# Token tile transposes, w_out rows and a scale chain at other places of one kernel's program order

## The chip, the core and the metric

The kernel runs on one core of a Trainium2 chip. Its engines work side by side, each through its own queue in order: PE (matrix products into PSUM), DVE and ACT (elementwise work, ACT also the GELU), POOL and SP (here mostly issuing transfers; ACT issues some too). The metric is the device time of one execution in microseconds (us). Times inside the profiled execution count from the start of its span.

## The reference

The input x has 2048 tokens of 576 channels. All is float32.

```python
h = _layernorm(x) * (1 + ca) + sa
x = x + ga * _A_ref(h, ...)              # a state-space convolution over the tokens
h = _layernorm(x) * (1 + cb) + sb
z = _gelu(einsum("bsd,df->bsf", h, w_in))          # 576 -> 4608
z1, z2 = z[..., :2304], _layernorm(z[..., 2304:])
g = einsum("ts,bsf->btf", w_sp, z2) + b_sp[None, :, None]   # 2048 x 2048 over the tokens
x = x + gb * einsum("bsf,fd->bsd", z1 * g, w_out)  # 2304 -> 576
```

The kernel computes each large product from float16 pairs: a tensor is split into a high part (a rounded copy, made by ACT) and a low part (the rest, made by DVE), and three products of the parts are summed.

## The kernel before

Three stages follow one another. The first, the state-space part, is not touched.

**The token stage** (`phase_a`) goes over 16 tiles of 128 tokens. For tile b:

- `ln2_rows(b)` (DVE) makes the normalized rows n; it runs two tiles ahead, and lets go the buffer of the token load `x1t`, for which the next load on SP (`x1_load`) waits.
- `turn(b)` (PE) transposes n in five pieces into `pt`, a PSUM tile of which there is one. `turn_hi(b)` (ACT, two instructions) copies it to the high part of `nt`, `turn_lo(b)` (DVE, two) makes the low part, and issues its store `n_d` on POOL. There are three nt.
- `z2_mm(b, h)` (PE) for h = 0 to 4: 14 products each of nt with a strip of w_in, into `pz`, of which there are six. The first four need the high part, and so do the next four; the low part comes after that.
- `z2_gelu(b, h)` (ACT) writes pz through the GELU to z. A tile's z takes two buffers of four, so that tile b's first GELU waits until the store of tile b - 2 (`z_d`) has landed.
- `z2_stats` and `roots` (DVE) make mean and scale (`nm`, `r`) of z; roots is a chain of some 17 tiny instructions, followed, for odd b, by `z2_diff`, which forms a difference of z's two halves. `z2_norm` (ACT) then normalizes z, and `z2_store` (POOL) stores it. For tile b - 1 all this runs inside tile b.

Between these, weights for later are prepared: `do(b, k)` runs the side jobs of tile b at place k. Place A0 stands ahead of a tile's first GELU; there ACT forms sums of squares of loaded weights (`wsst`, `wst`), and waits for their loads. The whole stage is pinned: each engine runs its instructions in the order in which the code names them.

After tile 15, its last statistics, roots, norm and store follow outside the loop.

**The first block** (`first_block`) makes the first 512 tokens of g. Its loop runs over nine column blocks f, called pairs here. For each pair PE multiplies w_sp with four sets, `zset` (set 4f + i), 42 products each (`g_products`); `part(f, i)` is the work of ACT and DVE that goes beside set i. A set is loaded from z_d into `raw`, gets three sums (DVE), a high part (ACT) and a low part (DVE, 2.0 us); there are three buffers, and the sets are made two ahead. Part 0 of a pair also takes the pair before through its sums (`gt`, six DVE instructions) and its product with z1. In pairs 1 to 6 PE has two units of z1 products besides (`ps<-n2q,wf`); four units stand ahead of pair 0. In the parts 1 to 3 rows of w_out are split, one a part (`wout_hi` on ACT, `wout_lo` on DVE, then the load of a later row on SP). The scales of the next block (`roots_sp(1)`, `scales_gate(1)`) are a chain of 20 tiny DVE instructions. ACT issues the stores of two sets out of three in its own queue (`set_d`), each behind the low part of its set.

After pair 8 the output product with w_out follows, and then three more blocks of the same kind; both are not touched.

The lines of the profile are those of a helper (L222) nearly everywhere, so instructions are told apart by their tiles.

Of the kernel before, what the change touches and what calls it, by code (L numbers as in the profile page):

```python
# [914 lines left out]
class Mlp:  # L915
# [466 lines left out]
    def phase_a(self):  # L1382
        self.n2o, self.n2t, self.wrs = {}, {}, {}
        self.prods, self.z1s, self.n2, self.bsp, self.gbs, self.wfs = {}, {}, {}, {}, {}, {}
        ap = self.ap = self.pool(self.c2, "ap", 2)
        cpa = ExitStack()
        self.pa = self.pool(cpa, "pa", 6, space=PSUM)
        self.ps1 = lambda: self.pa.tile([128, 512], F32, name="pz")
        self.zp = self.pool(self.c2, "zp", 2)
        self.wp = self.pool(self.ctx, "wp", 7, side="right")  # L1390

        self.bq = self.pool(self.ctx, "bq", 1, side="right")
        self.cfp = self.ctx.enter_context(ExitStack())
        self.fp = self.pool(self.cfp, "fp", 1, side="right")
        self.wso = ap.tile([128, 4, 10, 128], F16, name="wso", bufs=1)
        self.nc, plain = self.tied, self.nc
        self.nc.vector.memset(self.wso[64:, :, 9], 0.0)

        LD, PE, A0, A1, V0, V1 = range(6)
        sides = [[[] for _ in range(6)] for _ in range(17)]  # L1400

        def side(b, k, fn, *a):
            sides[b][k].append((fn, a))

        def do(b, k):
            for fn, a in sides[b][k]:
                fn(*a)

        for q in range(5):
            side(2 * q, LD, self.side_load, q)  # L1410
            side(2 * q + 1, A0, self.side_sum, q)
            side(2 * q + 1, PE, self.win_scale, q)
            side(2 * q + 1, A1, self.side_hi, q)
            side(2 * q + 1, V1, self.side_last, q)
            side(2 * q + 1, V1, self.side_lo, q, 0)
            side(2 * q + 2, V0, self.side_lo, q, 1)
        for h in range(2):
            side(1, LD, self.bsp_load, ap, h)
            side(2, A0, self.norm_bsp, h)
        for i in range(8):  # L1420
            side(2 + i // 2, A1, self.wsp_load, 0, i, ap)
            side(3 + i // 2, A0, self.norm_sp, 0, i)
        for i in range(12):
            side(6 + i // 2, A1, self.out_load, ap, i)
            side(7 + i // 2, A0, self.norm_out, i)
        for i in range(6):
            side(12 + i // 2, A1, self.wsp_load, 1, i, ap)
            side(13 + i // 2, A0, self.norm_sp, 1, i)
        side(13, V1, self.sums_out)
        side(14, PE, self.scales_out)  # L1430
        side(6, V1, self.sums_sp, 0)
        side(7, PE, self.scales_sp, 0)
        side(11, PE, self.scales_gate, 0)
        side(12, PE, self.scale_p, 0)
        for i in range(7):
            side(9 + i, V0, self.wsp_sums, i)
            side(9 + i, A1, self.wsp_hi, 0, i)
            side(9 + i, V1, self.wsp_lo, 0, i)
            side(8 + i, V1, self.block_load, 0, i)
        side(12, LD, self.z1_rows, 0)  # L1440
        side(14, LD, self.bias_load, 0)
        for f, b in ((0, 14), (9, 15), (1, 15)):
            side(b, LD, self.z1_load, 0, f)


        self.turn(0)
        self.turn_hi(0)
        self.x1_load(4)
        self.turn_lo(0)
        do(0, LD)  # L1450
        self.z2_mm(0, 0)
        do(0, A0)
        self.z2_gelu(0, 0)
        self.ln2_rows(1)
        do(0, PE)
        self.z2_mm(0, 1)
        self.z2_gelu(0, 1)
        self.start_sum(4)
        self.z2_mm(0, 2)
        self.turn(1)  # L1460
        self.start_lo(3)
        self.win_scale(9)
        self.turn_hi(1)
        self.start_hi(4)
        self.turn_lo(1)
        do(0, V0)
        self.z2_gelu(0, 2)
        self.z2_mm(0, 3)
        do(0, A1)
        self.start_lo(4)  # L1470
        self.ln2_rows(2)
        self.z2_stats(0, 0, 1, 2, 3)
        self.z2_gelu(0, 3)
        self.ln2_stats(3)
        do(0, V1)
        self.z2_stats(0, 4)
        self.z2_mm(0, 4)
        self.z2_gelu(0, 4)
        for b in range(1, 16):
            do(b, LD)  # L1480
            self.z2_mm(b, 0)
            do(b, A0)
            self.z2_gelu(b, 0)
            self.z2_stats(b - 1, 5)
            self.roots(b - 1, b + 2 if b + 2 < 16 else None)
            if b % 2:
                self.z2_diff(b - 1)
            self.z2_norm(b - 1)
            if b + 2 < 16:
                self.ln2_rows(b + 2)  # L1490
            if b + 4 < 16:
                self.x1_load(b + 4)
            self.z2_mm(b, 1)
            if b + 1 < 16:
                self.turn(b + 1)
            do(b, PE)
            self.z2_gelu(b, 1)
            self.z2_store(b - 1)
            do(b, V0)
            self.z2_stats(b, 0, 1)  # L1500
            if b + 1 < 16:
                self.turn_hi(b + 1)
            if b + 1 < 16:
                self.turn_lo(b + 1)
            self.z2_mm(b, 2)
            self.z2_gelu(b, 2)
            do(b, A1)
            self.z2_mm(b, 3)
            self.z2_stats(b, 2, 3)
            self.z2_gelu(b, 3)  # L1510
            if b + 3 < 16:
                self.ln2_stats(b + 3)
            do(b, V1)
            self.z2_stats(b, 4)
            self.z2_mm(b, 4)
            self.z2_gelu(b, 4)
        cpa.close()
        self.z2_stats(15, 5)
        self.roots(15)
        self.z2_norm(15)  # L1520
        self.z2_store(15)
        self.nc = plain
        self.c2.close()
# [497 lines left out]
    def first_block(self, order):  # L2021
# [16 lines left out]
        def sums(n):  # L2038
            if n < 36:
                self.z2_sums(n)  # L2040
# [13 lines left out]
        def part(f, i):  # L2054

            n = 4 * f + i
            if i == 0 and f:
                gate[:] = self.g_unit(0, f - 1, pgs.pop())
                gate[0]()
                hi(n + 2)  # L2060
                lo(n + 2)
                load()
                gate[1]()
                if f < 7:
                    z1()
                    z1()
                gate[2]()
                store(n + 2)
                sums(n + 4)
            if i:  # L2070
                if i == 1 and f:
                    gate[3]()
                if 2 <= f < 8:
                    k = next(rows)
                    self.wout_hi(k)
                    self.wout_lo(k)
                if f:
                    sums(n + 4)
                if (f, i) == (0, 3):
                    z1()  # L2080
                    z1()
                hi(n + 2)
                if i == 1 and f:
                    gate[4]()
                if not f:
                    sums(n + 3)
                lo(n + 2)
                load()
                store(n + 2)
                if i == 1 and f in (4, 5):  # L2090
                    self.wss[f + 2] = self.bp.tile([128, 2, 512], F32, name="gt", bufs=1).rearrange("p h (k n) -> p (h k) n", n=256)
                    self.wsp_read(self.wss[f + 2], 1, f + 2)
                if (f, i) == (0, 3):
                    sums(n + 4)
                if (f, i) == (8, 2):
                    self.next_first(1)

# [31 lines left out]
        sums(3)  # L2129
        for f in range(9):  # L2130
            part(f, 0)
            if f == 1:
                self.wout_load(0)
                self.wout_load(1)
            if f == 6:
                self.total_sp(1, self.bank())
            if f == 8:
                self.roots_sp(1)
                self.scales_gate(1)
                self.cfp.close()  # L2140
                self.fp = self.pool(self.ctx, "fq", 1, side="right")
                self.n2_load(1, 0)
                self.block_read(1, 0)
                self.next_loads(1)
            pgs.append(self.g_products(0, f))
            if f == 4 or f == 5:
                self.norm_sp(1, f + 2)
            if f == 5:
                self.sums_sp(1)
            if f == 7:  # L2150
                self.gate_load(0)
# [89 lines left out]
```

## Time and profile before

| | |
|---|---|
| median of 3 runs | 1720.89 us (1719.2 to 1723.23) |
| the profiled execution | 1718.49 us, span 1716.7 us |
| PE busy | 1625.4 us (95%) |
| DVE busy | 1252.5 us (73%) |
| ACT busy | 834.5 us (49%) |
| token stage, loop | about 390 to 632 us |
| first block, PE's products | about 642 to 857 us |

How to read the rows: a row of the timeline has the start, the time for all instructions of the row, the engine, the line, the operation, what it writes and reads, shapes, the count, and in brackets how long the engine stood before it and what ended that. A row of the waits has the engine and tile, what it waited for, us in total, times, and the longest. In a row of stretches stand the stretch, its length, the busy time of each engine with the number of instructions, then the clock that PE was granted (1.00 is full speed), the share of the transfer engines and the rate. A PE row's length includes the last product's own pipeline, so that two rows may overlap by some 0.16 us.

### The profile page before, as it was taken

Reading aid. Unit: us, or ns where it says so; the run is one execution under the profiler, and the core shown is the slowest. Engines: PE = TensorE matmul, PEld = TensorE weight load, DVE = VectorE, ACT = ScalarE, POOL = GpSimd, SP = SyncE. Lnnn points to the kernel's source line nnn. Section 1 sums busy time; section 2 is a strip of 40 time slices with the busy share of each in tenths; the row PEclk is TensorE's granted clock in tenths of the full one; section 3 lists DMA queues with packets and bytes.
Section 4 is the critical chain, followed back from the end, with each engine's and each line's share of the span. In section 5 each row is a group of like instructions: output and inputs, shape, how many; then the busy total and the mean of one; then the engine's idle time right before and its main releaser. Section 6 shows DMA issues by size and latency. Waiting matters only on the chain.

```text
span 1716.7 us, 39681 instructions
## 1 busy us (share of the span) xinstructions
PE 1625.4 (95%) x16838; PEld 1241.5 (72%) x16838; DVE 1252.5 (73%) x2251; ACT 834.5 (49%) x1239; POOL 211.5 (12%) x340
## 2 busy tenths in 40 slices
PE   3778999969999999999999999999999999999999
PEld 1345667754554447778778888888888888888887
DVE  7897899988989987888997777795443486343442
ACT  7899999844676564455433443332321142112210
POOL 3251111122222110000000000000111100111100
PEclk9778999989999999999999999999999999999999
DMA  8666646796887897776647877665667563556521
GB/s 249 164 214 189 194 133 185 204 281 203 267 267 245 235 277 275 250 256 240 228 144 248 308 264 268 232 208 182 224 214 244 193 212 105 205 198 213 193 98 42
DMA packets 179490, 367.08 MB, mean 214 GB/s; under 512 B 37952, under 2 KB 101824, under 8 KB 178544
## 3 DMA queue, kind: packets, MB, share of 16 engines
q1 hardware_dynamic: 138304, 168.56, 32.6%
q0 software_dynamic: 34528, 169.11, 29.5%
q10 hardware_dynamic: 6480, 26.86, 3.8%
q8 instruction: 132, 2.16, 0.5%
q14 instruction: 46, 0.38, 0.1%
HBM read 263.18 MB, written 101.31 MB: 212 GB/s over the span
## 4 chain that ended last, share of the span: by engine, by line
PE 67%; DVE 19%; DMA 5%; ACT 4%; issue 4%; POOL 1%; SPq 0%; ACTq 0%; DVEq 0%; POOLq 0%
PE ps L222 58%; PE pz L222 3%; PE pk_c L222 1%; PE pk_b L222 1%; PE pk_d L222 1%; DVE bsz L222 1%; PE pk_a L222 1%; DVE zset L222 1%; DVE zz_a L222 1%; DMA zset<-set_d 1%; DVE n L222 1%; DVE pg_b L222 1%; DVE gt L222 1%; DVE zz_b L222 1%; DMA wsst<-in_w_spT 1%
## 5 line engine op out<-in xcount | busy, mean ns | idle before, releaser
L222 PEld LDWEIGHTS <-zset 128*128 128x128 f16 x7182 | 702.8, 98 | 92.0 <-DVE zset L222 7.2
L222 PE MATMUL ps<-wsp,zset 128*128 128x256 f16 x6048 | 669.0, 273 | 6.2 <-DVE zset L222 5.5
L222 PE MATMUL pz<-wz,nt 128*128 128x512 f16 (+1 forms) x1120 | 223.3, 359 | 8.5 <-ACT nt L222 5.4
L222 ACT ACTIVATE z<-gt 128x1024 f16<-128x1024 f32 x56 | 59.0, 1054 | 283.0 <-DVE gt L222 283.0
L222 PEld LDWEIGHTS <-nt 128*128 128x128 f16 x1120 | 109.2, 99 | 116.9 <-ACT nt L222 7.2
L222 DVE SCALAR_TENSOR_TENSOR gt<-ps,sc,bsp 128x512 f32<-128x512 f32 x36 | 27.0, 749 | 205.3 <-PE ps L222 203.6
L222 PE MATMUL ps<-wout,z 128*128 128x288 f16 x1344 | 170.0, 286 | 0.0
L1949 POOL DMA_DIRECT2D zset<-set_d x96 | 51.1, 532 | 868.8 <-PE ps L222 616.1
L222 PEld LDWEIGHTS <-z 128*128 128x128 f16 x1344 | 131.5, 98 | 33.0
L222 PE MATMUL ps<-n2o,zset 128*128 128x256 f16 x1134 | 128.2, 273 | 0.0
L222 DVE SCALAR_TENSOR_TENSOR gt<-ps,sc,gt 128x512 f32<-128x512 f32 (+1 forms) x180 | 122.2, 696 | 7.6
L222 DVE TENSOR_TENSOR raw<-raw 128x512 f32<-128x512 f32 (+2 forms) x228 | 119.1, 528 | 11.1 <-DMA raw<-z_d 6.8
L222 ACT ACTIVATE zset<-raw 128x1792 f16<-128x1792 f32 x48 | 81.2, 1691 | 59.6 <-PE ps L222 30.9
L222 DVE TENSOR_TENSOR zset<-raw,zset 128x1792 f16<-128x1792 f32 x48 | 97.0, 2020 | 15.8 <-ACT zset L222 15.8
L222 DVE TENSOR_TENSOR z<-ps,z 128x512 f32<-128x512 f32 (+1 forms) x126 | 72.0, 599 | 36.8 <-ACT z L222 26.7
L222 ACT ACTIVATE wsp<-raw,sc 128x1792 f16<-128x1792 f32 x25 | 44.6, 1785 | 42.7 <-DVE raw L222 35.0
L222 ACT ACTIVATE z<-pz,sc 128x512 f32<-128x512 f32 (+1 forms) x96 | 51.7, 583 | 19.7 <-PE pz L222 10.3
L222 ACT ACTIVATE z<-z,sc 128x1024 f32<-128x1024 f32 x21 | 24.1, 1148 | 75.6 <-DVE z L222 71.9
L222 ACT ACTIVATE z<-z,nm,r 128x1152 f32<-128x1152 f32 x24 | 31.5, 1342 | 52.1 <-DVE nm L222 29.7
L222 PE MATMUL ps<-n2q,wf 128*128 128x512 f16 x252 | 55.7, 379 | 0.0
L222 PE MATMUL ps<-wout,z1b 128*128 128x288 f16 x384 | 52.4, 286 | 0.0
L222 DVE SCALAR_TENSOR_TENSOR wsp<-raw,sc,wsp 128x1792 f16<-128x1792 f32 x25 | 52.0, 2078 | 0.0
(727 smaller groups left out, 2634.0 us busy)
## 6 DMA issues: line engine op xcount, KB each, us to landing
zset<-set_d POOLq DMA_DIRECT2D x96, 896.0 KB, 4.9
raw<-z_d SPq DMA_DIRECT2D x48, 512.0 KB, 5.6
set_d<-zset ACTq DMA_DIRECT2D x24, 896.0 KB, 6.0
z_d<-z POOLq DMA_DIRECT2D x32, 576.0 KB, 9.5
zset<-wa_d POOLq DMA_DIRECT2D x18, 896.0 KB, 4.9
raw<-in_w_spT SPq DMA_DIRECT2D x25, 512.0 KB, 4.4
set_d<-zset SPq DMA_DIRECT2D x12, 896.0 KB, 5.4
wst<-in_w_in SPq DMA_DIRECT2D x8, 1024.0 KB, 9.8
```

Of the source, the lines that this page charges most:

```text
L222: return self.tc.keep_in_program_order(f(*a, **k))
L1949: self.nc.gpsimd.dma_start(o, self.set_d[f, j - 1] if j else self.wa_d[f])
```

## The change

In the token stage, `turn(b + 1)` goes from behind the second product of tile b to behind its first; `turn_hi(b + 1)` goes from behind the second GELU and the first statistics to directly behind the first GELU; `turn_lo(b + 1)` goes to directly behind roots. In the first block, the two first w_out loads are issued in pair 0 instead of pair 1, and the rows are split in the pairs 1 to 6 instead of 2 to 7. The scale chain goes from the start of pair 8 to the end of part 3 of pair 6.

```diff
         for b in range(1, 16):
             do(b, LD)
             self.z2_mm(b, 0)
+            if b + 1 < 16:
+                self.turn(b + 1)
             do(b, A0)
             self.z2_gelu(b, 0)
+            if b + 1 < 16:
+                self.turn_hi(b + 1)
             self.z2_stats(b - 1, 5)
             self.roots(b - 1, b + 2 if b + 2 < 16 else None)
+            if b + 1 < 16:
+                self.turn_lo(b + 1)
             if b % 2:
                 self.z2_diff(b - 1)
             self.z2_norm(b - 1)
...
             self.z2_mm(b, 1)
-            if b + 1 < 16:
-                self.turn(b + 1)
             do(b, PE)
             self.z2_gelu(b, 1)
             self.z2_store(b - 1)
             do(b, V0)
             self.z2_stats(b, 0, 1)
-            if b + 1 < 16:
-                self.turn_hi(b + 1)
-            if b + 1 < 16:
-                self.turn_lo(b + 1)
             self.z2_mm(b, 2)
...
-                if 2 <= f < 8:
+                if 1 <= f < 7:
                     k = next(rows)
                     self.wout_hi(k)
                     self.wout_lo(k)
...
+                if (f, i) == (6, 3):
+                    self.roots_sp(1)
+                    self.scales_gate(1)
...
-            if f == 1:
+            if f == 0:
                 self.wout_load(0)
                 self.wout_load(1)
             if f == 6:
                 self.total_sp(1, self.bank())
             if f == 8:
-                self.roots_sp(1)
-                self.scales_gate(1)
                 self.cfp.close()
```

DVE in tile 5 of the token stage, from the end of roots (nm of tile 4) to tile 5's statistics. z_5932 and z_5933 are the halves of tile 4's z, z_6082 is the first half of tile 5's. Before:

```order
L222 SCALAR_TENSOR_TENSOR nm_6105<-mvx,r_6104 128x1
L222 TENSOR_TENSOR z_5932<-z_5933,z_5932 128x1152
L222 SCALAR_TENSOR_TENSOR n_6111<-x1t,mvx,mrow 128x576
L222 SCALAR_TENSOR_TENSOR n_6111<-n_6111,rx,mrow 128x576
L222 COPY n_6111<-n_6111 128x64
...
L222 BN_STATS bsz<-z_6082 128x6 x2
L222 TENSOR_TENSOR nt<-pt,nt 128x512
L222 TENSOR_TENSOR nt<-pt,nt 64x128
```

and now (the buffers have new numbers):

```order
L222 SCALAR_TENSOR_TENSOR nm_6114<-mvx,r_6113 128x1
L222 TENSOR_TENSOR nt<-pt,nt 128x512
L222 TENSOR_TENSOR nt<-pt,nt 64x128
L222 TENSOR_TENSOR z_5938<-z_5939,z_5938 128x1152
L222 SCALAR_TENSOR_TENSOR n_6123<-x1t,mvx,mrow 128x576
L222 SCALAR_TENSOR_TENSOR n_6123<-n_6123,rx,mrow 128x576
L222 COPY n_6123<-n_6123 128x64
...
L222 BN_STATS bsz<-z_6088 128x6 x3
```

The two nt instructions stand ahead of the difference, the next rows and the statistics now. ACT in the same tile, before:

```order
L222 ACTIVATE wso,acc<-wst 128x2560
L222 ACTIVATE wsst,acc<-wsst 128x1024 x2
L222 ACTIVATE z_6082<-pz,sc 128x512
L222 ACTIVATE z_5933<-z_5933,nm_6105,r_6104 128x1152
L222 ACTIVATE z_5932<-z_5932,r_6104 128x1152
L222 ACTIVATE z_6082<-pz,sc 128x512
L222 ACTIVATE nt<-pt 128x512
L222 ACTIVATE nt<-pt 128x128
```

and now:

```order
L222 ACTIVATE wso,acc<-wst 128x2560
L222 ACTIVATE wsst,acc<-wsst 128x1024 x2
L222 ACTIVATE z_6088<-pz,sc 128x512
L222 ACTIVATE nt<-pt 128x512
L222 ACTIVATE nt<-pt 128x128
L222 ACTIVATE z_5939<-z_5939,nm_6114,r_6113 128x1152
L222 ACTIVATE z_5938<-z_5938,r_6113 128x1152
L222 ACTIVATE z_6088<-pz,sc 128x512
```

The copies stand behind the first GELU, which itself stands behind the sums of squares of that tile. DVE at the end of pair 6 of the first block, from the last w_out row to pair 7's first sums, now:

```order
L222 SCALAR_TENSOR_TENSOR wout<-gbs,sc,wout 128x576
L222 TENSOR_TENSOR raw<-raw 128x256
L222 TENSOR_TENSOR raw<-raw 128x512
L222 TENSOR_TENSOR zset<-raw,zset 128x7x256
L222 TENSOR_SCALAR sc<-sc 128x1
L222 TENSOR_SCALAR p2e<-sc 128x1
...
L222 TENSOR_SCALAR sc<-p2h 128x1
L222 SCALAR_TENSOR_TENSOR gt<-ps,sc,bsp 128x512
L222 SCALAR_TENSOR_TENSOR gt<-ps,sc,gt 128x512
```

The chain (sc, p2e, p2h) stood behind the product gt<-gt,sc,z1b of pair 8 before; set 29 (zset) and the first sums (gt<-ps,sc,bsp) followed each other directly.

## The prediction

> **What bounds the kernel now.** I read the page first (PE busy 95% of the span, DVE 73%), then the waits by stage. The change touches two stages: the token stage (390 to 636 us of the span) and the first block behind it (to 857). These are PE's two largest waits in the token stage loop (us in total, times, longest), DVE's largest there, and the busy time of the engines (span of the stretch, PE, PEld, DVE, ACT).
>
> ```profile
> PE pz L222 <- ACT nt L222: 4.7, 5, 1.8
> PE pz L222 <- DVE nt L222: 2.6, 2, 1.7
> ...
> DVE bsz L222 <- ACT z L222: 3.8, 2, 2.4
> ...
> 403.00:632.00 229.00, 221.22 (x1175) 115.04 (x1175) 207.51 (x626) 155.78 (x246) 48.61 (x63) 1.00 0.83 251
> ```
>
> PE waits 7.3 us for nt, the transposed tile, which is what the first edit goes for. But DVE is the engine that never rests: 207.5 us busy in 229 with 626 short instructions (the rest is mostly gaps of a few hundredths between them), and with one wait worth the name, 3.8 us for ACT's z. PE stands because DVE is late, and DVE's stream decides when the stage ends. The rows at the seam to the next block show it (start, us, engine, what, idle before):
>
> ```profile
> 629.58 12.25 PE L222 MATMUL ps<-n2q,wf 128*128 128x512 f16 x56
> 642.64 4.76 PE L222 MATMUL ps<-wsp,zset 128*128 128x256 f16 x42 [0.59 <-DVE zset L222]
> 648.70 9.13 PE L222 MATMUL ps<-wsp,zset 128*128 128x256 f16 x82 [1.29 <-DVE zset L222]
> ...
> 636.36 2.58 ACT L222 ACTIVATE z<-z,nm,r 128x1152 f32<-128x1152 f32 x2 [5.43 <-DVE nm L222]
> 640.56 2.03 DVE L222 TENSOR_TENSOR zset<-raw,zset 128x1792 f16<-128x1792 f32 x1 [1.61 <-ACT zset L222]
> ```
>
> ACT waits for DVE's last nm (636.3), normalizes, makes set 0; DVE finishes it at 642.6; PE, which has filled 12 us with z1 products, waits for just that. An earlier PE would wait longer here. From set 1 on PE runs on its own work until 833.
>
> **Edit 1, the token stage.** It adds and removes no instruction. On DVE turn_lo (two nt instructions) goes from behind the statistics to directly behind roots. On ACT turn_hi goes directly behind the tile's first GELU. DVE runs its queue in order, so from now on everything behind roots waits for that GELU. Where was ACT at that moment? Below are DVE's next instruction after roots in tiles 3, 5, 7 and 9, and ACT's first GELU of the same tiles; for tile 5 also the load that ACT stood for last, the two waits that DVE has there today, and the copies' lengths.
>
> ```profile
> 443.79 1.36 DVE L222 TENSOR_TENSOR z<-z,z 128x1152 f32<-128x1152 f32 x1
> 471.06 1.36 DVE L222 TENSOR_TENSOR z<-z,z 128x1152 f32<-128x1152 f32 x1
> 502.57 1.36 DVE L222 TENSOR_TENSOR z<-z,z 128x1152 f32<-128x1152 f32 x1
> 531.66 1.36 DVE L222 TENSOR_TENSOR z<-z,z 128x1152 f32<-128x1152 f32 x1
> ...
> 443.83 0.69 ACT L222 ACTIVATE z<-pz,sc 128x512 f32<-128x512 f32 x1 [1.41 <-DMA z_d<-z]
> 475.55 1.06 ACT L222 ACTIVATE wsst<-wsst 128x1024 f32<-128x1024 f32 x1 [0.80 <-DMA wsst<-in_w_spT]
> 476.60 0.67 ACT L222 ACTIVATE z<-pz,sc 128x512 f32<-128x512 f32 x1
> 479.56 0.67 ACT L222 ACTIVATE z<-pz,sc 128x512 f32<-128x512 f32 x1
> 480.12 0.75 ACT L222 ACTIVATE nt<-pt 128x512 f16<-128x512 f32 x2
> 502.13 0.69 ACT L222 ACTIVATE z<-pz,sc 128x512 f32<-128x512 f32 x1 [1.27 <-PE pz L222]
> 532.00 0.69 ACT L222 ACTIVATE z<-pz,sc 128x512 f32<-128x512 f32 x1 [2.60 <-DMA z_d<-z]
> ...
> 477.30 0.56 DVE L222 BATCH_NORM_STATS2 bsz<-z 128x6 f32<-128x384 f32 x1 [1.37 <-ACT z L222]
> 480.26 0.56 DVE L222 BATCH_NORM_STATS2 bsz<-z 128x6 f32<-128x384 f32 x1 [2.40 <-ACT z L222]
> 480.91 1.02 DVE L222 TENSOR_TENSOR nt<-pt,nt 128x512 f16<-128x512 f32 x2
> ```
>
> A copy starts 0.56 behind its GELU (479.56, 480.12) and its first half takes about 0.45 of the 0.75, so turn_lo can start 1.0 behind the GELU's start. Against DVE's arrival:
> - tile 3: 443.83 + 1.0 - 443.79 = 1.0;
> - tile 5: 476.60 + 1.0 - 471.06 = 6.5. The 1.37 + 2.40 that DVE stands there now falls away behind it: 2.8 net. A delay from tile 3 is absorbed here, if the transfer that ACT waits for lands no later;
> - tile 7: 502.13 + 1.0 - 502.57 = 0.6; tile 9: 532.00 + 1.0 - 531.66 = 1.3.
>
> In the other tiles ACT is there first (it waits for nm, as at 636.36), so the move costs nothing: the 1.02 us are DVE's either way. With tile 3 inside tile 5's: 2.8 + 0.6 + 1.3 = 4.7 us on a stream with no slack.
>
> Two transfers move with it. SP issues the next token load when ln2_rows lets the buffer go, and the norm loads behind it:
>
> ```profile
> 460.92 0.89 SPq L222 DMA_DIRECT2D wsst<-in_w_spT  x2
> n_d<-nt POOLq DMA_DIRECT2D x16, 288.0 KB, 7.9
> ```
>
> ln2_rows now stands behind turn_lo (1.0) and tile 3's wait (1.0), so tile 5's norm loads go out 2 us later, 3.1 with a wait in tile 4. The second took over 13 us (460.92 to 475.55), so they lie in a backlog that may swallow this: 0 to 3.1, I take 1.0. On POOL the n_d store now precedes the z_d store whose landing frees ACT's GELU in tiles 7 and 9. 288 KB at the stretch's 251 GB/s are 1.1 us each: 0 to 1.1, I take 0.4, since n_d goes out over a microsecond earlier. Given back: the wait below, as ACT has the copies behind it by then.
>
> ```profile
> 616.89 2.08 DVE L222 SCALAR_TENSOR_TENSOR wsp<-xz,sc,wsp 128x1792 f16<-128x1792 f32 x1 [0.34 <-ACT wsp L222]
> ```
>
> Edit 1: 4.7 + 1.0 + 0.8 - 0.3 = **+6.2 us** (4.4 to 10). The 7.3 us of PE's waits buy nothing: tile 15's nt comes 5 us earlier in DVE's order and 6 later on the clock, so PE ends the stage near 630 again and waits 6 to 7 us at 642 instead of 0.6. A slow clock behind that wait (priced below, at most 1.7) mostly falls into the wait of 1.29 at 648.7: +0.2.
>
> **Edits 2 and 3, the first block.** First the rate at which PE runs undisturbed, then the block's end:
>
> ```profile
> 674.33 18.50 PE L222 MATMUL ps<-wsp,zset 128*128 128x256 f16 x168
> 692.67 6.21 PE L222 MATMUL ps<-n2q,wf 128*128 128x512 f16 x28
> ...
> 796.39 37.32 PE L222 MATMUL ps<-wsp,zset 128*128 128x256 f16 x338
> 834.00 9.34 PE L222 MATMUL ps<-wsp,zset 128*128 128x256 f16 x84 [0.29 <-DVE zset L222]
> 851.40 6.21 PE L222 MATMUL ps<-wsp,zset 128*128 128x256 f16 x40 [2.71 <-DVE zset L222]
> 851.00:856.00 5.00, 4.60 (x27) 3.43 (x28) 4.59 (x10) 1.78 (x2) 0.00 (x0) 0.66 0.89 260
> ...
> 819.61 2.01 DVE L222 TENSOR_TENSOR zset<-raw,zset 128x1792 f16<-128x1792 f32 x1
> 826.88 2.02 DVE L222 TENSOR_TENSOR zset<-raw,zset 128x1792 f16<-128x1792 f32 x1
> 830.13 0.82 DVE L222 SCALAR_TENSOR_TENSOR wout<-xo,sc,wout 128x576 f16<-128x576 f32 x1 [1.24 <-ACT wout L222]
> 844.98 0.15 DVE L222 TENSOR_SCALAR sc<-sc 128x1 f32<-128x1 f32 x1
> 848.20 1.22 DVE L222 TENSOR_TENSOR gt<-gt,z1b 128x1024 f32<-128x1024 f32 x1
> 849.33 2.02 DVE L222 TENSOR_TENSOR zset<-raw,zset 128x1792 f16<-128x1792 f32 x1
> ```
>
> A pair of column blocks ("pair" from here on: one f of the loop) has 168 products, and takes 692.67 - 674.33 = 18.34 us, 0.109 each. The last three pairs, 6 to 8, begin at 796.4 and would end at 851.4; PE ended at about 857.4 (851.40 + 6.21 less the last product's tail). So 6.0 us are there to be had: waits, and a last 40 products at a granted clock of 0.66. DVE is late. The edits take three w_out rows (0.8 each, one with a wait of 1.24: 3.7) out of pair 7. The scale chain (3.2 us: 844.98 to the subtraction at 848.2) is not removed but put ahead of pair 7's first sums, in the same saturated stream. So set 30 (819.61) ends at 824.8, and PE, in pair 7 from 814.7, wants it 84 products in, at 823.9: a new wait of 0.9. Set 31 (826.88) ends 3.2 - 0.7 later, at 831.4, and PE wants it at 829.4: 2.0. In pair 8 ACT's copy of the product (1.1 us, as the two halves at 873.39 below) has no chain to hide under, and set 32 must wait for ACT's store issue. I get set 35 at 850.7 instead of 851.35, PE wanting it 1 us earlier, and the block's end at 855.3: 2.1 gained. Bounds: nothing (set 35's own gain is 0.65, and the clock could fall again) and 6.0 (all of it).
>
> By the Trainium skill, TensorE: Matmul & The Clock Gate, Part 1, the clock falls after an idle window of about 3.4 us. The trace shows 0.66 after a wait of 2.71, so the measured row decides here. By the page alone the slow stretch would have another cause and stay, and the sum below would be about 1 us higher.
>
> What takes part of it back is the output product, which needs pair 8's product:
>
> ```profile
> 873.39 1.13 ACT L222 ACTIVATE z1b<-gt 128x512 f16<-128x512 f32 x2
> 874.35 3.10 PE L222 MATMUL ps<-wout,z1b 128*128 128x288 f16 x24
> ```
>
> It is ready at 874.5; PE wants it 6 products after 874.35, at 875.2. DVE's chain to it starts behind set 35, 0.65 earlier; PE comes 2.1 earlier: it waits 0.8. Edits 2 and 3: -2.1 + 0.8 = **-1.3 us**. Three rows in pair 1 and two loads of 288 KB in pair 0 I cost at nothing: PE has z1 products in pairs 1 to 6 and stood for no set between 657 and 833. Without that cover they would cost the same 3.7.
>
> **Sum**: 6.2 + 0.2 - 1.3 = +5.1. The profiled execution took 1718.49 (span 1716.7, 1.8 around it), so 1723.6 by its time. It lies 2.4 under the median of the runs; from 1720.89 it makes **1726.0**.
>
> **Rivals.** *PE's waits are the price.* If DVE's waits behind roots do not come (ACT there in time), PE's 7.3 us and the block's 6.0 are gained: 1720.9 - 13.3 = 1707.6, or 1714.9 with the block's alone. It decides once ACT reaches the first GELU 1.0 us before roots ends in tiles 3 to 9. For it: those are PE's only waits. Against: DVE has no idle time in which to end earlier, and four tiles miss that point in the rows above. 15%.
>
> *A draw.* Transfers land a little earlier for a later DVE, the token stage loses 4.4 and less, and the block gives back most of its 6.0: -1.6 to +2, about 1720.5. For it: DVE's lag behind PE at pair 7 is only 0.6, and a smaller lag there frees more. Against: the chain moved within a full stream. 22%.
>
> **How the numbers follow.** The forecast has 63%, with a range of its own of 1722.5 (4.4 lost, 2.8 given back) to 1731 (10 lost, nothing given back). The range of 1718.5 to 1731 takes in the draw and leaves the gain out. 0.2% (3.4 us) is about what a measurement of this kernel can tell from no change: under 1717.5 faster, over 1724.3 slower. Of the forecast's 63%, 57 lie over that and 6 within; of the draw 17 within, 3 over, 2 under; of the gain 12 under, 3 within. Faster 14%, within 26%, slower 60%.
>
> **What would show it.** Right: DVE nt waits for ACT nt in tiles 3, 5, 7 and 9, the longest some 6 us; the last nm comes 5 to 7 us later than 636.3 and PE stands as long before set 0; at the block's end waits on sets 30 and 31, and no 0.66 clock. Wrong: the last nm at 636 or before, or no DVE wait at nt; then the gain or the draw holds. If set 35 meets PE without a wait, the block's step is wrong.

## The result, and the profile after

| | before | changed |
|---|---|---|
| median of the runs, us | 1720.80 (1717.97 to 1726.44, 6 runs) | 1738.72 (1737.31 to 1742.95, 6 runs) |
| span of the profiled execution, us | 1716.7 | 1735.5 |
| ratio of the times, 95% interval | | 1.0104 (1.0084 to 1.0123) |

The change costs 17.9 us by the medians, where 5.1 were forecast. The sign was right, the size was not: 1738.7 lies far above the range.

The seam between the two stages first, in the timeline of the changed kernel (start us, us, engine, what, idle before): ACT's last normalization, PE's rows around it, and PE at the end of the first block.

```profile
624.77 18.11 PE L222 MATMUL pz<-wz,nt 128*128 128x512 f16 x97
647.42 9.23 PE L222 MATMUL ps<-n2q,wf 128*128 128x512 f16 x42 [1.52 <-ACT z L222]
653.17 2.59 ACT L222 ACTIVATE z<-z,nm,r 128x1152 f32<-128x1152 f32 x2 [5.44 <-DVE nm L222]
657.40 0.39 PE L222 MATMUL ps<-wsp,zset 128*128 128x256 f16 x2 [0.75 <-ACT zset L222]
659.46 15.38 PE L222 MATMUL ps<-wsp,zset 128*128 128x256 f16 x124 [1.67 <-DVE zset L222]
...
813.40 27.89 PE L222 MATMUL ps<-wsp,zset 128*128 128x256 f16 x254
841.90 4.76 PE L222 MATMUL ps<-wsp,zset 128*128 128x256 f16 x42 [0.61 <-DVE zset L222]
848.45 13.93 PE L222 MATMUL ps<-wsp,zset 128*128 128x256 f16 x126 [1.78 <-DVE zset L222]
863.38 4.76 PE L222 MATMUL ps<-wsp,zset 128*128 128x256 f16 x42 [1.01 <-DVE zset L222]
869.32 4.54 PE L222 MATMUL ps<-wsp,zset 128*128 128x256 f16 x40 [1.17 <-DVE zset L222]
873.69 5.31 PE L222 MATMUL ps<-wout,z 128*128 128x288 f16 x42
891.98 2.38 PE L222 MATMUL ps<-wout,z1b 128*128 128x288 f16 x18 [0.48 <-ACT z1b L222]
```

The normalization stood at 636.36, now at 653.17: +16.8 us, so nearly all of the loss is made in the token stage. The first block gives back a little: from pair 6's start to the first w_out product it was 857.44 - 796.39 = 61.05 us, and is 873.69 - 813.40 = 60.29.

Absolute times of two executions are not quite comparable: the stages ahead of the token loop end at other times from one execution to the next. So below a token stage is measured from the first to the last nm row, nm being the last small DVE instruction of roots, one for each tile. These are the two rows of before, and then those of the changed kernel:

```profile
416.44 0.16 DVE L222 SCALAR_TENSOR_TENSOR nm<-mvx,r 128x1 f32<-128x1 f32 x1
...
636.10 0.16 DVE L222 SCALAR_TENSOR_TENSOR nm<-mvx,r 128x1 f32<-128x1 f32 x1
```

```profile
415.72 0.16 DVE L222 SCALAR_TENSOR_TENSOR nm<-mvx,r 128x1 f32<-128x1 f32 x1
...
652.92 0.16 DVE L222 SCALAR_TENSOR_TENSOR nm<-mvx,r 128x1 f32<-128x1 f32 x1
```

219.7 us before, 237.2 after: +17.5. Where DVE stood is in the changed kernel's waits of the stage and, behind the dots, in its timeline:

```profile
DVE nt L222 <- ACT nt L222: 18.7, 6, 6.3
ACT wsst L222 <- DMA wsst<-in_w_out: 16.1, 6, 5.1
ACT wsst L222 <- DMA wsst<-in_w_spT: 13.1, 7, 4.2
...
445.92 1.02 DVE L222 TENSOR_TENSOR nt<-pt,nt 128x512 f16<-128x512 f32 x2 [2.76 <-DMA z_d<-z]
463.59 1.02 DVE L222 TENSOR_TENSOR nt<-pt,nt 128x512 f16<-128x512 f32 x2 [1.73 <-ACT nt L222]
481.23 1.01 DVE L222 TENSOR_TENSOR nt<-pt,nt 128x512 f16<-128x512 f32 x2 [6.27 <-ACT nt L222]
497.77 1.02 DVE L222 TENSOR_TENSOR nt<-pt,nt 128x512 f16<-128x512 f32 x2 [0.60 <-ACT nt L222]
513.49 1.00 DVE L222 TENSOR_TENSOR nt<-pt,nt 128x512 f16<-128x512 f32 x2 [4.27 <-ACT nt L222]
546.30 1.02 DVE L222 TENSOR_TENSOR nt<-pt,nt 128x512 f16<-128x512 f32 x2 [3.77 <-ACT nt L222]
580.95 1.02 DVE L222 TENSOR_TENSOR nt<-pt,nt 128x512 f16<-128x512 f32 x2 [2.07 <-ACT nt L222]
```

These are the waits at turn_lo in tiles 3, 4, 5, 6, 7, 9 and 11, 21.5 us together. The 3.8 us that DVE stood in tile 5 before are gone: 17.7 net, which is the loss. ACT's waits for the weight-norm loads (wsst) are what lies behind most of them; they are 13.1 and 16.1 us now, and before they were:

```profile
ACT wsst L222 <- DMA wsst<-in_w_spT: 8.8, 3, 4.4
ACT wsst L222 <- DMA wsst<-in_w_out: 1.0, 2, 0.7
```

Why are the loads late? Take tile 7's. They are issued on SP in tile 6 (w_out pieces, two of them), and ACT reads them in tile 7. First before, then the changed kernel:

```profile
491.00 0.16 DVE L222 SCALAR_TENSOR_TENSOR nm<-mvx,r 128x1 f32<-128x1 f32 x1
492.36 1.47 SPq L222 DMA_DIRECT2D wsst<-in_w_out  x2
492.89 1.01 POOL L222 DMA_DIRECT2D z_d<-z  x1 [5.14 <-ACT z L222]
499.83 0.93 ACT L222 ACTIVATE wsst<-wsst 128x864 f32<-128x864 f32 x1
```

```profile
497.01 0.16 DVE L222 SCALAR_TENSOR_TENSOR nm<-mvx,r 128x1 f32<-128x1 f32 x1
499.32 0.54 POOL L222 DMA_DIRECT2D n_d<-nt  x1 [5.54 <-ACT z L222]
499.85 2.01 POOL L222 DMA_DIRECT2D z_d<-z  x2
500.11 0.88 SPq L222 DMA_DIRECT2D wsst<-in_w_out  x2
511.21 0.92 ACT L222 ACTIVATE wsst<-wsst 128x864 f32<-128x864 f32 x1 [5.07 <-DMA wsst<-in_w_out]
```

Before, the loads went out from 1.36 us behind nm on, the first of them ahead of the stores, and ACT's second read found its data without a wait 8.8 us behind nm. Now they go out 3.1 us behind nm, behind the n_d store and the first of the two z_d stores, and the second load lands 14.2 us behind nm. 1.7 us at the issue have become at least 5.4 at the landing. The experiments have to show what of this is the cause.

### The profile page after: what moved, and what is told of

Read it like the earlier page. It is cut to its first block, busy times and chain, and to the rows that moved or that the text cites. A ratio compares the mean times of both kernels' runs of the same rounds, so it can differ in the third digit from the quotient of the medians.

```text
span 1735.5 us, 39688 instructions
## 1 busy us (share of the span) xinstructions
PE 1626.5 (94%) x16838; PEld 1236.0 (71%) x16838; DVE 1252.0 (72%) x2251; ACT 835.1 (48%) x1239; POOL 209.9 (12%) x340
## 3 DMA queue, kind: packets, MB, share of 16 engines
q0 software_dynamic: 34528, 169.11, 29.2%
## 4 chain that ended last, share of the span: by engine, by line
PE 62%; DVE 19%; DMA 8%; issue 5%; ACT 4%; POOL 1%; SPq 0%; ACTq 0%; DVEq 0%; POOLq 0%
PE ps L222 55%; DMA zset<-set_d 2%; DMA z_d<-z 1%; DVE zz_a L222 1%; PE pk_b L222 1%; PE pk_a L222 1%; PE pk_d L222 1%; DVE pg_a L222 1%; DVE bsz L222 1%; PE pz L222 1%; DVE pg_b L222 1%; PE pk_c L222 1%; DVE n L222 1%; DVE zset L222 1%; ACT z L222 1%
## 5 line engine op out<-in xcount | busy, mean ns | idle before, releaser
L222 PE MATMUL pz<-wz,nt 128*128 128x512 f16 (+1 forms) x1120 | 225.9, 361 | 13.1 <-ACT nt L222 4.5
L222 DVE TENSOR_TENSOR raw<-raw 128x512 f32<-128x512 f32 (+2 forms) x228 | 119.2, 529 | 10.9 <-DMA raw<-z_d 6.6
```

Source lines behind the costliest of these rows:

```text
L222: return self.tc.keep_in_program_order(f(*a, **k))
```

## Experiments

Ratios are against the kernel before on the same chip, with 95% intervals; 0.1% is 1.7 us. "Stage" is first to last nm, in the run's profiled execution. The same code repeats it to 0.1 us from tile to tile but for tile 5's w_sp loads, which make it 217.3 to 221.5 in four runs of the old order.

### Which edit

**Edit 1 alone.**

```
 for b in range(1, 16):          # before + the loop of the changed kernel
...
+    self.turn(b + 1)            # behind z2_mm(b, 0)
+    self.turn_hi(b + 1)         # behind z2_gelu(b, 0)
+    self.turn_lo(b + 1)         # behind roots
```

> Edit 1 alone (token stage), the first block as before. The changed kernel's last nm came 16.8 us late (653.17 against 636.36 in ACT's row at the seam) and its block end moved by about -0.8, its output product by +0.5. So if edit 1 is the whole loss: +17 us against before (15.5 to 18.5), DVE standing some 19 us at turn_lo for ACT's copy. If the two other edits hold a part of the loss behind the block (the three DMA waits near the end are longer in the changed kernel), it is 14 or less.

1735.01 us, ratio 1.0084 (1.0061 to 1.0107), stage 236.0. DVE stands 20.3 us at turn_lo. By the ratio that is +14.5 us (10.5 to 18.4), by the stage +16.3 of the 17.5: edit 1 is the loss, or nearly all of it.

**Edits 2 and 3 alone, then each by itself.**

```
-                if 2 <= f < 8:
+                if 1 <= f < 7:          # edit 2, with the two loads at f == 0
...
+                if (f, i) == (6, 3):    # edit 3, and gone at f == 8
+                    self.roots_sp(1)
+                    self.scales_gate(1)
```

> Edits 2 and 3 alone, the token stage as before. By the forecast -1.3 us (-2.1 at the block's end, +0.8 at the output product); read from the changed kernel's trace -0.8 + 0.5 = -0.3. If they hold a part of the loss: +2 or more. In the trace: sets 30 and 31 waited for by 0.6 to 0.9 and 1.8 to 2.0 us, no clock of 0.66 at the block's last 40 products.

> Edit 2 alone: w_out rows a pair sooner, the scale chain at its old place in pair 8. By the forecast's own terms the chain in pair 6 makes the new waits on sets 30 and 31 (2.9 us; measured 0.6 + 1.8), and the rows taken out of pair 7 free 3.7 us. So without the chain: no wait on sets 30 and 31, set 35 waited for by 0 to 1.5 us, w_out products starting 59.0 us or less behind pair 6's start (before 61.05, changed kernel 60.29); -2 us, hard to tell in the time. If the rows are hidden anyway and the chain's place is all: the 2.7 us wait on set 35 stays.

> Edit 3 alone: the scale chain (3.2 us on DVE) at the end of pair 6's last part, w_out rows as before. From edits 2 and 3 together (60.34 us from pair 6's start to the w_out products, with the last 40 products at full clock) and edit 2 alone (60.07 with them at 0.66, 58.4 without) the chain costs 1.9 there. So without the rows' move: waits on sets 30 and 31 of 1.6 and 2.8 or more (the forecast's 0.9 and 2.0 and the 0.7 that two rows ahead of them take), 62 us and more at one clock, +1 to +2, which the time can hardly show. If the chain is a gain by itself (set 35's wait of 2.7 goes and nothing comes): 57 to 59 us.

| | time, ratio | pair 6's start to w_out, us | PE's waits there, us | last 40 products, us |
|---|---|---|---|---|
| before (profile) | 1 | 61.05 | 0.29 + 0.58 + 2.71 | 6.21 |
| both | 0.9999 (0.9983 to 1.0015) | 60.34 | 0.61 + 1.78 + 1.07 + 1.17 | 4.54 |
| rows only | 0.9994 (0.9972 to 1.0016) | 60.07 | 0.32 + 2.72 | 6.21 |
| chain only | 1.0006 (0.9988 to 1.0024) | 61.07 | 0.61 + 2.34 + 0.73 | 4.54 |

No time differs from before. The traces are finer (the columns of the table are PE's rows in the timeline, read as in the rows of the changed kernel above). 6.21 against 4.54 for the last 40 products is the clock (1.67 us). The run of the chain alone has its slow clock elsewhere, behind its wait on set 31:

```profile
833.75 20.18 PE L222 MATMUL ps<-wsp,zset 128*128 128x256 f16 x168 [2.34 <-DVE zset L222]
```

The same count took 18.50 us at full clock (the row at 674.33 of before), so 1.68 of its 61.07 are the clock. Without the clock's part the times are: before 59.38, rows only 58.40, chain only 59.39, both 60.34. So the rows alone gain 1.0 us, the chain alone changes nothing, and the two together lose 1.0: beside the rows the chain costs 1.9. Why they don't add is open. My expectation for the rows alone was wrong in one point: set 35's wait of 2.7 stays, so it is not the rows of pair 7 that make set 35 late but the chain that stands right ahead of it in pair 8. My expectation for the chain alone gave 62 us and more at one clock; it was 59.39.

### What in edit 1

The edits from here on are shown against edit 1 alone, where nothing else is said.

**turn_lo back at its old place.** Transposes and ACT's copies stay early.

```
             self.roots(b - 1, b + 2 if b + 2 < 16 else None)
-            if b + 1 < 16:
-                self.turn_lo(b + 1)
...
             self.z2_stats(b, 0, 1)
+            if b + 1 < 16:
+                self.turn_lo(b + 1)
```

> Edit 1 without DVE's part: transposes and ACT's copies go early as in the change, turn_lo (DVE's two subtractions and the n_d store) stays behind the statistics of the tile's first GELUs, as before. If DVE's standing at turn_lo is the loss, it is gone: -3 to +2 us against before, DVE's waits at nt under 2 us, PE's waits for nt near the 7.3 us of before. If PE's earlier transposes (a wait of PE for n at the turn, 5.4 us in 5 times in the changed kernel) or ACT's earlier copies are the loss, +8 or more stays.

1720.05 us, ratio 1.0000 (0.9984 to 1.0015), stage 218.3, no wait of DVE at nt. PE's early transposes and ACT's early copies cost nothing; turn_lo's place is the loss. PE's waits for nt were 6.0 us, all for DVE, so the early copies had not helped PE either.

**ACT's copies ahead of the norm jobs and the GELU.**

```
             if b + 1 < 16:
                 self.turn(b + 1)
+                self.turn_hi(b + 1)
             do(b, A0)
             self.z2_gelu(b, 0)
-            if b + 1 < 16:
-                self.turn_hi(b + 1)
```

> Edit 1 alone with ACT's two copies of the next transposed tile (turn_hi) put ahead of the tile's norm jobs and first GELU. ACT then no longer stands for a norm load or for z_d ahead of the copies, so DVE finds nt ready at turn_lo. If DVE's standing there behind ACT's loads is the loss: DVE's waits at nt fall from 20 us to under 4, the norm loads go out early again, and the time is -3 to +4 against before. If the first GELU, held up in turn by the copies, is what DVE needs next, waits for ACT's z take the place: +6 or more.

1721.01 us, ratio 1.0006 (0.9986 to 1.0026), stage 219.1. turn_lo is as early as in the change, and DVE has no wait at nt at all. ACT still stands 5.3 us for one norm load (in tile 11), and that costs DVE nothing, since ACT has made the copies by then. So DVE stood at turn_lo for what ACT had queued ahead of the copies.

**The n_d store at its old place.** turn_lo's two instructions stay early, its store goes behind the z_d store again.

```
-                self.turn_lo(b + 1)
+                self.turn_lo(b + 1, False)     # without its store
...
             self.z2_stats(b, 0, 1)
+            if b + 1 < 16:
+                self.turn_store(b + 1)         # POOL: n_d <- nt
```

> Edit 1 alone, but the store of the transposed tile (n_d, 288 KB) stays at its old place on the store queue, behind the z_d store; turn_lo's two DVE instructions stay early. In edit 1's trace the norm loads of tile 7 take over 11 us from issue to landing (before: under 7.5), and n_d goes out 0.8 us ahead of them. Transport theory (n_d ahead of the loads is what makes them land late): the loads land 1.1 us sooner in every tile (288 KB at about 260 GB/s), and as each wait feeds the next, the loss of edit 1 (+14 here, 1735.0) falls to between +6 and +11. Issue theory (the loads are late because they are issued behind DVE's wait and meet the z_d stores): no more than 2 us are gained, +12 to +15 stay.

1738.05 us, ratio 1.0107 (1.0071 to 1.0143), stage 236.7, 21.2 us of DVE's waits at nt. Nothing gained: n_d's place is not the cause.

**The norm loads ahead of the token load**, with edit 1, and without it.

```
-            if b + 4 < 16:
-                self.x1_load(b + 4)
...
             do(b, A1)                    # issues the norm loads
+            if b + 4 < 16:
+                self.x1_load(b + 4)
```

> Edit 1 alone, with one more move: SP issues the token load x1t (which must wait for ln2_rows on DVE, now behind turn_lo) behind the tile's weight-norm loads instead of ahead of them. The norm loads then go out once ACT has used the two wsst buffers, 4 to 6 us earlier than in the changed kernel (494 instead of 500.1 in tile 6). Loop theory (each wait of DVE at turn_lo delays ln2_rows, so the token load, so the norm loads behind it on SP, so ACT's first GELU of the next tile, so the next wait at turn_lo): ACT's waits for wsst fall from 29 us to 8 or less, DVE's at nt from 18.7 to 8 or less, and the loss from +17 to between +3 and +8. Plain theory (DVE's waits stand each for itself, at ACT's GELU behind z_d and at loads that are slow wherever they are issued): waits of 14 us and more remain, +13 or more.

> The kernel before, with only the one move of the run with the loads first: SP issues the norm loads ahead of the token load. It says what this move is worth without edit 1, and so what edit 1 is worth once the loads are on time. In the trace of before DVE lost 3.8 us to late loads, in tile 5 alone: -2 to -4 expected (stage 216 instead of 219.7 between the first and the last nm). If the run with the loads first, which came out at no change, hides a cost of edit 1 that this move pays for, the gain here is larger: -6 or more.

With edit 1: 1720.62 us, ratio 0.9994 (0.9973 to 1.0014), stage 218.0. One order of two loads on SP takes the whole loss away, more than I expected. The waits of its stage, where no wait for wsst is left on ACT:

```profile
DVE nt L222 <- ACT nt L222: 2.2, 4, 1.2
...
PE pz L222 <- DVE nt L222: 0.2, 1, 0.2
```

PE's waits for nt are gone too, and the stage is no shorter for it: they never were the price of anything.

Without edit 1: 1718.50 us, ratio 0.9984 (0.9962 to 1.0006), stage 215.5; tile 5's waits are gone, 4.1 us of the stage. So with the loads on time edit 1 still costs 218.0 - 215.5 = 2.4 us of stage. It gains nothing under any of these conditions.

### Why the loads land late

After this I took it for a loop: a wait at turn_lo delays ln2_rows, which delays the token load, which delays the norm loads behind it on SP, and these make the next wait.

**Loads first up to tile 5 only.**

```
-            if b + 4 < 16:
+            if b >= 6 and b + 4 < 16:
                 self.x1_load(b + 4)
...
             do(b, A1)
+            if b < 6 and b + 4 < 16:
+                self.x1_load(b + 4)
```

> Edit 1 alone with the norm loads ahead of the token load up to tile 5 only (they serve tiles up to 6); from tile 6 on the loads stand behind the token load, as in edit 1. Loop theory (a wait in one tile makes the next one, so without the first there are no later ones): tiles 7, 9 and 11 lose at most the forecast's 0.6, 1.3 and 0, nm-to-nm times are those of before to 0.6 us, +1 to +4 against before. Each-tile theory (turn_lo, 1.0 us ahead of ln2_rows, puts the loads behind the z_d stores in every tile by itself): tiles 7, 9 and 11 stand 4.3, 3.8 and 2.1 us as in the changed kernel, and the loss is about half of edit 1's: +6 to +10.

1731.14 us, ratio 1.0054 (1.0035 to 1.0074), stage 227.6. The loop theory falls. Tile 6 has no wait here, and tile 7 has its full one all the same; it, tile 9 and tile 11 stand 4.33, 4.07 and 2.54 us (changed kernel: 4.27, 3.77, 2.07). Tile 7's rows:

```profile
493.22 0.16 DVE L222 SCALAR_TENSOR_TENSOR nm<-mvx,r 128x1 f32<-128x1 f32 x1
494.84 0.54 POOL L222 DMA_DIRECT2D n_d<-nt  x1 [4.86 <-ACT z L222]
495.38 1.01 POOL L222 DMA_DIRECT2D z_d<-z  x1
495.63 2.17 SPq L222 DMA_DIRECT2D wsst<-in_w_out  x2
506.80 0.92 ACT L222 ACTIVATE wsst<-wsst 128x864 f32<-128x864 f32 x1 [1.84 <-DMA wsst<-in_w_out]
509.07 1.00 DVE L222 TENSOR_TENSOR nt<-pt,nt 128x512 f16<-128x512 f32 x2 [4.33 <-ACT nt L222]
```

Without any wait ahead, turn_lo's own 1.02 us ahead of ln2_rows put the loads 2.4 us behind nm instead of 1.36, so behind the n_d store and the first z_d store; the second landed 13.6 us behind nm, where before it was there at 8.8.

**ln2_rows ahead of turn_lo.**

```
+            if b + 2 < 16:
+                self.ln2_rows(b + 2)
             if b + 1 < 16:
                 self.turn_lo(b + 1)
             if b % 2:
                 self.z2_diff(b - 1)
...
-            if b + 2 < 16:
-                self.ln2_rows(b + 2)
```

> Edit 1 alone, but DVE does ln2_rows ahead of turn_lo (roots, ln2_rows, turn_lo, difference). turn_lo is still early (1.85 us later than in edit 1), but the token load's buffer, and with it the norm loads, comes free 1.35 us behind nm as before, not 2.4. Order theory (turn_lo's 1.0 us ahead of ln2_rows puts the norm loads behind the z_d stores, and they land 4 us later for it: in the run with the loads first up to tile 5, tile 7's loads went out 2.4 us behind nm and landed 13.6 behind it, before 1.36 and at most 8.8): the loads of tiles 7 and 9 land at most 9.5 us behind nm, DVE's waits at nt in tiles 7, 9 and 11 fall to 1 us and less, and the loss to between 0 and +4. Position theory (turn_lo so early meets ACT's first GELU late wherever the loads go): waits of 2 us and more in these tiles (4.3, 3.8 and 2.1 less 1.85), +6 or more.

1724.55 us, ratio 1.0025 (1.0005 to 1.0045), stage 221.3. Tile 7's rows and, behind the dots, two of the stage's waits:

```profile
493.32 0.16 DVE L222 SCALAR_TENSOR_TENSOR nm<-mvx,r 128x1 f32<-128x1 f32 x1
494.67 1.32 SPq L222 DMA_DIRECT2D wsst<-in_w_out  x2
496.74 0.54 POOL L222 DMA_DIRECT2D n_d<-nt  x1 [6.66 <-ACT z L222]
497.27 2.01 POOL L222 DMA_DIRECT2D z_d<-z  x2
501.60 0.92 ACT L222 ACTIVATE wsst<-wsst 128x864 f32<-128x864 f32 x1
...
DVE bsz L222 <- ACT z L222: 4.3, 4, 1.2
DVE nt L222 <- ACT nt L222: 0.7, 1, 0.7
```

The loads go out 1.35 us behind nm, ahead of the stores, and are there 8.3 behind it. One wait of 0.7 at nt is left, although turn_lo is only 1.85 us later than in the change, less than the 4.3 it stood in tile 7. Outside tile 5 DVE stands 3.2 of the 4.3 us at the statistics for ACT's z, where before it stood none; with the 0.7 that is most of the 4.5 us by which these tiles take longer. The order theory holds.

What the loads meet on the way stands in the trace's DMA queues (q1 has SP's transfers, q0 POOL's). These are the MB that each moved, in stretches counted from tile 6's nm:

| | 2 to 7 us: SP, POOL | 7 to 13 us: SP, POOL |
|---|---|---|
| before | 1.00, 0.02 | 0.13, 1.85 |
| changed | 0.84, 0.57 | 0.49, 1.53 |
| loads first up to tile 5 | 0.44, 0.72 | 0.71, 1.26 |
| ln2_rows ahead of turn_lo | 1.10, 0.30 | 0.04, 1.65 |

Where the loads are early, nearly all of them is through before POOL's stores take the engines. Where they are late, 0.5 to 0.7 MB is left for the stretch in which the stores take the larger part. It is not the order of issue alone: before, the row of the two loads (492.36, 1.47 long) also reaches past the issue of the first z_d store at 492.89, but POOL's queue moved only 0.02 MB up to 498. How much of the delay is z_d and how much n_d is not shown: moving n_d back gained nothing, and no run moved the z_d stores by themselves.

By the Trainium skill, Trainium Kernel Development and Optimization, Key Constraints, DMAs from the SP, ACT and POOL queues all run on the same 16 DMA engines and interleave. These rows agree: a store issued on POOL holds up a load issued on SP.

**Late loads in the old order**, two runs. The first issues the n_d store on SP, ahead of the norm loads:

```
-                self.turn_lo(b + 1)
+                self.turn_lo(b + 1, False)
...
+            if b + 1 < 16:
+                self.turn_store(b + 1)         # SP: n_d <- nt
             do(b, A1)
```

> The order of before on all engines, but SP issues the n_d store (POOL did) ahead of the norm loads, so the loads wait for turn_lo behind the statistics and go out some 4 us later (496.3 instead of 492.4 in tile 6), behind the z_d stores. If late loads cost only because turn_lo stands in front (DVE reaches ACT's first GELU output 5 us later in the old order): ACT's waits for wsst grow from 10 to over 20 us, but DVE loses little, 0 to +6. If late loads cost by themselves, whatever the order on DVE: +10 or more.

1762.51 us, ratio 1.0229 (1.0194 to 1.0264), stage 258.0: a miss for the theory, and a badly chosen delay. The loads of tile 3 went out 13.7 us behind nm, not some 5, because here a true loop closed: loads late, ACT late, its copies late, turn_lo late, and behind turn_lo the next loads. Late by that much, the loads cost in the old order on DVE too. So the second run has a milder delay: two wso instructions of DVE go ahead of ln2_rows.

```
+            if b in (2, 4, 6, 8):
+                self.side_lo(b // 2 - 1, 1, 1)   # DVE's part; its stores stay in V0
             if b + 2 < 16:
                 self.ln2_rows(b + 2)
...
```

> The order of before, turn_lo at its old place, with one move on DVE: in tiles 2, 4, 6 and 8 the two wso instructions (1.41 us) go ahead of ln2_rows instead of behind it, their stores as before. So the norm loads go out 2.8 us behind nm instead of 1.36, as late as the changed kernel's, with nothing else late. Order theory: they land some 4 us later (13 us behind nm instead of 9) and ACT's waits for wsst grow from 10 to 15 us and more; DVE in the old order wants ACT's first GELU only 6.7 us behind nm in odd tiles, so it loses 0 to 3 us in all. If late loads cost whatever the order on DVE, as the run with the loads behind n_d suggests (there they went out 13 us behind nm): +6 or more. If 1.4 us at the issue do not move the landing: ACT's waits stay at 10 us and the explanation of the 4 us is wrong.

1723.10 us, ratio 1.0011 (0.9993 to 1.0030), stage 221.0. Tile 7's rows and, behind the dots, ACT's waits for wsst in the stage:

```profile
498.34 0.86 SPq L222 DMA_DIRECT2D wsst<-in_w_out  x2
505.55 0.92 ACT L222 ACTIVATE wsst<-wsst 128x864 f32<-128x864 f32 x1 [1.83 <-DMA wsst<-in_w_out]
506.60 0.92 ACT L222 ACTIVATE wsst<-wsst 128x864 f32<-128x864 f32 x1
...
ACT wsst L222 <- DMA wsst<-in_w_spT: 9.5, 4, 2.9
ACT wsst L222 <- DMA wsst<-in_w_out: 7.3, 4, 3.6
```

nm stood at 495.66, so the loads went out 2.7 us behind it and the second was there 10.9 behind it at the latest: about 2 us late (in tile 9 it was 3.3), not the 4 I expected. Here one of the two z_d stores went out ahead of them and n_d behind them; that the fewer bytes ahead are the reason is not shown. ACT waits 16.8 us for wsst, as much as expected, and DVE loses little: tile 7's step from nm to nm is 17.7 us as before, tile 9's 20.1 instead of 19.0, tile 3's 18.9 instead of 15.9. So 16.8 us of such waits on ACT cost 0 to 4 us where turn_lo stands behind the statistics; in the changed kernel 29.2 us of them, with turn_lo ahead, go with a loss of 17.

### A version that beats both

Loads first (no edit 1) and rows a pair sooner (no edit 3):

> The kernel before with the two parts that looked like a gain: norm loads ahead of the token load on SP (no edit 1) and w_out rows a pair sooner (edit 2, no edit 3). Stage between the first and the last nm 215.5 us (before 219.7, and 217.3 to 221.5 in repeats of the same code), block end 1.0 us sooner (w_out products 60.07 behind pair 6's start, before 61.05). If the two add: -3 to -5 us against before. If late rows of the first block take the earlier stage back: 0 to -2.

1717.64 us, ratio 0.9974 (0.9956 to 0.9991): 4.5 us under before, 1.5 to 7.6 by the interval. Stage 215.5, 59.90 us from pair 6's start to w_out. It is the only version here whose interval lies wholly below 1, and it is one of fourteen; the trace's two shorter stretches support it.

## Why the prediction was wrong, and where it was right

- **DVE decides, PE's waits buy nothing**: right. With the loads first PE's waits for nt fall to almost nothing and the stage does not shorten. So the rival falls by which they are the price.
- **DVE will stand at turn_lo for ACT**: right, and tile 5 to 0.2 us (6.5 forecast, 6.27 measured). That close a hit is luck: counted from the first nm, DVE came there 4.5 us later than before (59.1 against 54.5) and ACT's load 4.0 us later (63.1 against 59.1), both more than forecast.
- **The step that failed** is the term for the transfers that move: "they lie in a backlog that may swallow this: 0 to 3.1, I take 1.0", for tile 5 alone. In tiles 7 and 9 I set DVE's arrival against ACT's old times, 0.6 and 1.3, and wrote that in the other tiles the move costs nothing. But turn_lo's 1.0 us delays the norm loads in every even tile, and in tiles 6, 8 and 10 they do not just slide by it: POOL's stores now move beside them, and the second load is there 4.5 to 5.4 us later behind nm than before. DVE's waits that follow were measured at 4.27, 3.77 and 2.07 in tiles 7, 9 and 11. With 2.76 and 1.73 in tiles 3 and 4 (1.0 and 0 forecast) and 0.60 in tile 6 the waits are 21.5 us instead of 9.4, net 17.7 instead of 4.7. The +6.2 of edit 1 was 17.5 in the changed kernel's stage.
- **n_d ahead of z_d, 0.8 us for tiles 7 and 9**: not seen there, where ACT's wait ahead of the copies is for a norm load. In tile 3, where it was not forecast, ACT's first GELU waits for z_d until 1.55 us behind nm (444.55) instead of 0.12, which is half of DVE's 2.76. With the n_d store moved back ACT has no wait for z_d there, but one of 5.34 us for a norm load (at 446.66), so nothing was gained.
- **"PE ends the stage near 630 again and waits 6 to 7 us at 642"**: wrong. PE ended at 642.7, held up with the tiles, and stood 1.52 + 0.75 + 1.67 = 3.9 us around the seam. The last nm came 16.8 us later, not 5 to 7.
- **Edits 2 and 3, waits**: sets 30, 31 and 35 were forecast at 0.9, 2.0 and 1.0, and came at 0.61, 1.78 and 1.17; a fourth, 1.01 on set 34, was missed.
- **Edits 2 and 3, size**: -2.1 forecast, -0.76 measured (60.29 against 61.05). All of that and more is the clock, 1.67 us: the waits grew from 3.58 to 4.57. As forecast no 0.66 followed, but the clock is no steady gain of the edit (below). At one clock the rows were worth 1.0 by themselves and the chain nothing, but together they lost 1.0, where I had the two gain 2.1. The output product waited 0.48 us (0.8 forecast).
- **Behind the block** the changed kernel's profile lost 2.5 us more: 861.8 us from the first w_out product to the end of the span against 859.3. 0.48 of it is the output product, 0.7 are waits for sets loaded from memory (1.33 against 0.63). With the same code from there on, the other runs took 859.3 to 860.5. What made the rest stays open.
- **The draw and the gain**: no run of edit 1 as it stands supports either. With turn_lo early, a time equal to before came only with the loads first or with ACT's copies ahead, for other reasons than the one given.

## What to carry to other kernels

When an instruction moves ahead on an in-order engine, list what it now delays behind it, down to the buffers that come free and the loads that wait for them, and ask of each load which transfers will now move beside it or ahead of it. A load's lateness is not the delay at its issue: 1 us there became 4 at the landing. And where an early consumer must wait for another engine, look at what that engine has queued ahead of the producer; moving the producer, or the loads, may be worth more than moving the consumer.

## What the runs showed of the hardware

The same wait of PE on set 35, 2.70 to 2.72 us, is followed by a granted clock of 0.66 in some executions and of 1.00 in others, with the same 40 products behind it. In the rows alone (846.5 to 851.5) and in edit 1 alone (869.5 to 874.5), the columns being span, PE, PEld, DVE, ACT, POOL busy, clock, DMA share and GB/s:

```profile
846.50:851.50 5.00, 4.71 (x28) 3.59 (x29) 4.58 (x10) 1.88 (x2) 0.00 (x0) 0.66 0.96 275
```

```profile
869.50:874.50 5.00, 4.67 (x43) 4.17 (x44) 4.58 (x10) 1.85 (x2) 0.05 (x1) 1.00 0.87 253
```

Of thirteen profiles with this wait the 40 products took 6.21 us in five (before among them), 5.95 to 6.07 in three, and 4.54 in five. The chain alone shows the same behind a shorter wait: after 2.34 us the granted clock was 0.63 from 834 to 837. By the Trainium skill, TensorE: Matmul & The Clock Gate, Part 1, the gate's window of about 3.4 us is free-running, so that the same kernel comes out differently from run to run; that agrees with this spread. The same part of the Trainium skill has the clock fall after an idle window of that length; that does not agree, as 2.7 us and 2.34 us were enough here. For a prediction it means that such a term, 1.7 us, comes in with a chance and not for certain.
